# Loading two row tiles as one pair, both halves of wv on ScalarE's queue behind a write of zeros, and v in another order

## The chip, the cores and the metric

The kernel runs on one core of a Trainium2 chip. The metric is the device time of one execution in microseconds (us); the time before is the median of 3 runs. One further execution was recorded by the hardware profiler; all times inside the kernel are from that one, counted from its first instruction.

## What is computed

x is 2048 rows of 512 (bf16). It is layer-normed and goes through two branches whose results are added to x: a linear attention with 32 heads of 16, and a gated product of 1792 columns.

```
def _A_ref(x, wqkv, w_phi, wo):
    ...
    q, k, v = qkv[0], qkv[1], qkv[2]
    pq = jnp.einsum("bhsd,hdf->bhsf", q, w_phi)
    pk = jnp.einsum("bhsd,hdf->bhsf", k, w_phi)
    phi_q = jnp.concatenate([_softmax(pq, axis=-1), _softmax(-pq, axis=-1)], axis=-1)
    phi_k = jnp.concatenate([_softmax(pk, axis=-1), _softmax(-pk, axis=-1)], axis=-1)
    kv = jnp.einsum("bhsf,bhsd->bhfd", phi_k, v)
    z  = jnp.einsum("bhsf->bhf", phi_k)
    num = jnp.einsum("bhqf,bhfd->bhqd", phi_q, kv)
    den = jnp.einsum("bhqf,bhf->bhq", phi_q, z)[..., None] + 1e-6
    ...
def _B_ref(x, w_gate, w_up, w_down):
    ...
    h = g * u
    return jnp.einsum("bsf,fd->bsd", h, w_down)
x = A_x
xn = _layernorm(x, axis=-1)
return x + _A_ref(xn, A_wqkv, A_w_phi, A_wo) + _B_ref(xn, B_w_gate, B_w_up, B_w_down)
```

Attention sums k and v over all rows, and the rest treats each row by itself. So any assignment of rows to tiles gives the same result, if the output rows go back to the same places.

## The kernel before

The 2048 rows are 16 tiles of 128 rows (one row per partition) in four groups of four; `xall` holds them all. The order of instructions on each engine is the order in which the program is written (a manual schedule), so what is written earlier on an engine's queue goes first.

**Loads.** x0 and x2 (tiles 0 and 2) and the second half of the weight `wv` (`dma_wv(2, DC)`, L84) are issued first on SyncE's queue (SP), in that order; x1 and the first half of `wv` on ScalarE's queue (ACT, L91 and L92); x3 on GpSimd's (POOL, L93). Behind them SP issues the first 256 columns of the two gate weights `wg` and `wu`, the small `wphi`, their next pieces, a transposing load of a weight, further rows of x, and the rest (L94 to L103).

**First four tiles.** TensorE (PE) runs warm-up matmuls on constants (L307 to L313) while the loads are under way. For tile n, the row sum is made (`sum_of` on VectorE for tiles 0 and 3; on ScalarE with an accumulating activation, L378, for 1 and 2), and `sub_sum` (VectorE, L338) writes 512 x - sum, the centred row. `lt` (L203) transposes it on PE in four 128x128 pieces and a copy (VectorE or ScalarE, L207) puts the pieces into `xnT`. `first_v` (L354, matmuls at L237) multiplies with `wv`: four matmuls, the first two with the first half of `wv`, the others with the second. The variance is taken later (`stats_of`, `scales_of`, L341 to L348, VectorE and GpSimd), and the scale is put on where v is copied out (`first_v_out`) and in the exponentials. Then GpSimd makes `bd`, the block-diagonal form of `w_phi` (`make_bd`, L213), and PE goes into the gated branch (`ffn`, L266: four g matmuls at L275, four u matmuls at L279 per unit), three units, before `fold(1, W1k)` (L226) multiplies `w_phi` into the weights of k and needs `bd`.

The order of the first four tiles is written out at L376 to L405. On PE it is: transposes of tile 0, of tile 1, v of tile 0 (first half of `wv`), transposes of tile 2, v of tiles 1 and 2 (first half), v of tile 0 (second half), transposes of tile 3, v of tiles 1 and 2 (second half), v of tile 3.

**The rest.** Tiles 4 to 15 are normalised by VectorE, GpSimd and ScalarE and transposed by DMA (`ln_block`); k's features, v and their sums kv alternate with units of the gated branch (L435 to L452); then queries, attention and the final products `fin` (L285), whose results SP writes to `out` (L302).

Of the kernel before, what the change touches and what calls it, by code (L numbers as in the profile page):

```python
# [21 lines left out]
def kernel(  # L22
# [12 lines left out]
    nc = tc.nc  # L35
    P = 128
    S, D = A_x.shape[-2], A_x.shape[-1]
# [3 lines left out]
    NT = S // P  # L41
    DC = D // P
# [4 lines left out]
    TT = GT * P  # L47
    E1 = DH + 1

    x_view = A_x.flatten_outer_dims().rearrange("(n p) d -> p n d", n=NT)  # L50
    out_view = out.flatten_outer_dims().rearrange("(n p) d -> p n d", n=NT)

    consts = ctx.enter_context(tc.tile_pool(name="consts", bufs=1))
    wpool = ctx.enter_context(tc.tile_pool(name="wpool", bufs=1))
# [2 lines left out]
    xall = xpool.tile([P, NT, D], BF16)  # L57
    wv = wpool.tile([P, DC, D], BF16)
# [9 lines left out]
    def dma_x(lo, hi, eng=nc.sync):  # L68
        eng.dma_start(out=xall[:, lo:hi, :], in_=x_view[:, lo:hi, :])
# [4 lines left out]
    def dma_wv(lo, hi, eng):  # L74
        eng.dma_start(out=wv[:, lo:hi, :],
                      in_=A_wqkv[lo * P:hi * P, 2 * D:3 * D].rearrange("(c p) f -> p c f", p=P))

    def dma_gu(lo, hi):
        dma_cols(nc.sync, wg, B_w_gate, lo, hi)
        dma_cols(nc.sync, wu, B_w_up, lo, hi)  # L80

    dma_x(0, 1)
    dma_x(2, 3)
    dma_wv(2, DC, nc.sync)  # L84

    ET = mybir.EngineType
    ctx.enter_context(tc.manual_schedule(engines={ET.PE, ET.DVE, ET.Activation, ET.Pool, ET.SP}))
    ones = nc.const_aps.tensor(1.0, [P, P], BF16)
    first = consts.tile([P, 1], BF16)
    nc.scalar.activation(out=first[:], in_=ones[:, 0:1], func=AF.Exp, scale=1.0)  # L90
    dma_x(1, 2, nc.scalar)  # L91
    dma_wv(0, 2, nc.scalar)  # L92
    dma_x(3, 4, nc.gpsimd)  # L93
    dma_gu(0, 2 * P)  # L94
    nc.sync.dma_start(out=wphi[:], in_=A_w_phi.rearrange("(c h) d f -> (h d) c f", c=DC))
# [27 lines left out]
    xnT = xpool.tile([P, DC, S], BF16)  # L123
# [22 lines left out]
    def bank(name, dt=F32, n=TT):  # L146
        return ps_s.tile([P, n], dt, name=name, tag="s")
# [52 lines left out]
        for i in range(GT):  # L200
            chores.append(lambda i=i: apply(i))

    def lt(n, lo=0, hi=DC, copy=nc.scalar.copy):  # L203
        tp = bank("tp", BF16).rearrange("p (c t) -> p c t", c=DC)
        for c in range(lo, hi):
            nc.tensor.transpose(out=tp[:, c, :], in_=xns[n][:, c * P:(c + 1) * P], identity=ident[:])  # L206
        copy(out=xnT[:, lo:hi, n * P:(n + 1) * P], in_=tp[:, lo:hi, :])  # L207

    bd = consts.tile([P, DC, 8, DH], BF16)

# [24 lines left out]
    def proj(ps, n, w, js=range(DC)):  # L235
        for j in js:
            nc.tensor.matmul(ps, lhsT=xnT[:, j, n * P:(n + 1) * P], rhs=w[:, j, :],  # L237
                             start=(j == 0), stop=(j == DC - 1))
# [46 lines left out]
    def fin(n, cuts=(0, D)):  # L285
        T, t4 = n // GT, n % GT
        for lo, hi in zip(cuts, cuts[1:]):
            w = hi - lo
            ps = bank("fin")[:, 0:w]
            for f in range(FC):  # L290
                nc.tensor.matmul(ps, lhsT=hTs[T][:, f, t4 * P:(t4 + 1) * P], rhs=wd[:, f, lo:lo + w],  # L291
                                 start=(f == 0), stop=False)
            for c in range(DC):
                nc.tensor.matmul(ps, lhsT=oTs[n][:, c, :], rhs=wo[:, c, lo:lo + w],  # L294
                                 start=False, stop=(c == DC - 1))
            o_sb = opool.tile([P, w], BF16, name=f"o_sb{w}")
            if n < GT:
                nc.vector.scalar_tensor_tensor(out=o_sb[:], in0=ps, scalar=r2[n][:], in1=xall[:, n, lo:lo + w],
                                               op0=ALU.mult, op1=ALU.add)
            else:  # L300
                nc.vector.tensor_tensor(out=o_sb[:], in0=ps, in1=xall[:, n, lo:lo + w], op=ALU.add)  # L301
            nc.sync.dma_start(out=out_view[:, n, lo:lo + w], in_=o_sb[:])  # L302


    warm = bank("warm")
# [1 line left out]
    def warm_up(k, reps=DC):  # L307
        for _ in range(k):
            nc.tensor.matmul(warm[:, 0:reps * P], lhsT=ones,
                             rhs=nc.const_aps.tensor(1.0, [P, reps * P], BF16), start=True, stop=True)  # L310

    warm_up(7)
    warm_up(2, 1)  # L313

    with tc.tile_pool(name="ps_k", bufs=1, space=PSUM) as ps_k:
        kvbank = [ps_k.tile([P, TT], F32, name=f"kv{b}") for b in range(2)]
# [20 lines left out]
        def sub_sum(n, tot, lo=0, hi=D):  # L337
            nc.vector.tensor_scalar(out=xns[n][:, lo:hi], in0=xall[:, n, lo:hi], scalar1=float(D), scalar2=tot[:],  # L338
                                    op0=ALU.mult, op1=ALU.subtract)
# [14 lines left out]
        def first_v(n, js):  # L354
            if n not in vps:
                vps[n] = kvbank[n][:] if n < 2 else bank("pv")
            proj(vps[n], n, wv, js)
# [15 lines left out]
        def sum_of(n):  # L373
            nc.vector.tensor_reduce(out=tots[n][:], in_=xall[:, n, :], axis=AX.X, op=ALU.add)  # L374
# [3 lines left out]
            nc.scalar.activation(out=junk[:], in_=xall[:, n, :], func=AF.Identity, accum_out=tots[n][:])  # L378
        sub_sum(0, tots[0], 0, D // 2)
        sub_sum(0, tots[0], D // 2, D)  # L380
        sub_sum(1, tots[1])
        lt(0, 0, 2, nc.vector.tensor_copy)
        lt(0, 2, DC, nc.vector.tensor_copy)
        lt(1, 0, 2)
        sub_sum(2, tots[2])
        lt(1, 2, DC, nc.vector.tensor_copy)
        first_v(0, (0, 1))
        lt(2, 0, 2)
        sum_of(3)
        lt(2, 2, DC, nc.vector.tensor_copy)  # L390
        sub_sum(3, tots[3])
        first_v(1, (0, 1))
        first_v(2, (0, 1))
        first_v(0, (2, 3))
        lt(3)
        first_v(1, (2, 3))
        first_v(2, (2, 3))
        for n in (2, 3, 0, 1):
            stats_of(n)
            scales_of(n, float(D))  # L400
# [58 lines left out]
    with tc.tile_pool(name="ps_ab", bufs=1, space=PSUM) as ps_ab, \  # L459
# [23 lines left out]
        for n in range(NT):  # L483
            attend(n)
            if n + 5 < NT:
                qproj(n + 5)
            if n < 2:
                ffn(2)
                continue
            fin(n - 2)  # L490
            if n >= 4:
                ffn(2)
        ffn(len(units))
        fin(NT - 2)
        fin(NT - 1, (0, 3 * P, D))


# [28 lines left out]
```

## Time and profile before

| what | before |
|---|---|
| median of 3 runs | 220.36 us (220.27 to 220.91) |
| the profiled execution | 220.46 us |
| its span, first to last instruction | 218.8 us |
| PE busy | 214.9 us (98%) |
| VectorE, ScalarE, GpSimd busy | 141.0, 89.2, 74.9 us |
| x0 issued, landed | 0.79 us, 3.24 us |
| first transpose on PE | 4.34 us |
| first matmul of the gated branch | 9.34 us |
| data moved by DMA | 19.91 MB |

A line of the profile names the engine, the line of the kernel, the operation, and the tile written with those read. PE is TensorE's matmuls, PEld its weight loads, DVE is VectorE, ACT ScalarE, POOL GpSimd, SP SyncE; a q behind the name means the engine's issuing side. In the chain of work that ended last, each piece is what the next one waited for. "Landed" is when the last part of a transfer has raised its semaphore.

### The profile page before, as it was taken

What the parts mean: (1) busy time and instruction counts of PE and PEld (TensorE: products, weight loads), DVE (VectorE), ACT (ScalarE), POOL (GpSimd) and SP (SyncE); (2) the same over time, 40 slices, a digit from 0 to 9 for tenths busy, and PEclk for the clock granted to TensorE, in tenths of its full rate; (3) what the DMA queues carried; (4) which work ended last, traced back from release to release, by engine and by line L of the source; (5) the groups of instructions that cost most, each with busy time, mean ns of one, the idle gap of its engine ahead of it and who ended that gap; (6) DMA issues with size and microseconds to landing.
All of it is one profiled execution on the core that took longest, in us unless ns stands there. A gap on an engine that the chain in (4) does not pass through costs nothing.

```text
span 218.8 us, 3493 instructions
## 1 busy us (share of the span) xinstructions
PE 214.9 (98%) x1291; PEld 103.1 (47%) x1291; DVE 141.0 (64%) x242; ACT 89.2 (41%) x159; POOL 74.9 (34%) x72
## 2 busy tenths in 40 slices
PE   8999999999999999999999999999999999999994
PEld 3444445454444444444544444444444444454443
DVE  4878867786598758576599773296655655454321
ACT  5545686569575875565435212141231322100000
POOL 4450843373357554636045333033123033000000
PEclk9999999999999999999999999999999999999999
DMA  5999996005202240202028355114461431412201
GB/s 198 286 297 372 372 219 136 2 0 51 48 0 49 51 94 2 48 3 48 1 43 105 76 114 114 37 24 96 96 70 30 95 72 28 96 48 72 69 30 48
DMA packets 48433, 19.91 MB, mean 91 GB/s; under 512 B 37504, under 2 KB 48384, under 8 KB 48416
## 3 DMA queue, kind: packets, MB, share of 16 engines
q1 hardware_dynamic: 47952, 19.16, 38.9%
q10 hardware_dynamic: 416, 0.39, 0.5%
q8 instruction: 10, 0.16, 0.3%
q0 software_dynamic: 48, 0.13, 0.2%
q14 instruction: 7, 0.06, 0.1%
HBM read 8.67 MB, written 2.10 MB: 49 GB/s over the span
## 4 chain that ended last, share of the span: by engine, by line
PE 97%; DMA 1%; DVE 1%; issue 0%
PE g L275 22%; PE fin L291 22%; PE u L279 22%; PE fin L294 6%; PE q L237 6%; PE k L237 6%; PE pv L237 6%; PE kv L331 2%; PE ab L465 2%; DMA xall<-in_A_x_dram 1%; PE kv L237 1%; PE tp L206 1%; PE pq L226 1%; DVE tot L374 0%; DVE xn L338 0%; DVE o_sb L301 0%
## 5 line engine op out<-in xcount | busy, mean ns | idle before, releaser
L275 PE MATMUL g<-xnT,wg 128*128 128x512 bf16 x224 | 57.5, 379 | 0.0
L279 PE MATMUL u<-xnT,wu 128*128 128x512 bf16 x224 | 57.5, 379 | 0.0
L254 POOL TENSOR_TENSOR phiq<-e,rsum 128x1024 bf16<-128x1024 f32 x16 | 30.9, 1933 | 63.5 <-DVE rsum L252 56.0
L283 DVE TENSOR_TENSOR hT<-u,g_sb 128x512 bf16<-128x512 f32 x56 | 37.0, 666 | 23.9 <-PE u L279 15.8
L282 ACT CAST g_sb<-g 128x512 bf16<-128x512 f32 x56 | 32.9, 587 | 46.8 <-PE g L275 46.5
L250 DVE TENSOR_REDUCE sums<-e 128x64 f32<-128x1024 f32 x32 | 38.9, 1216 | 20.1 <-ACT e L247 20.1
L291 PE MATMUL fin<-wd,hT 128*128 128x512 bf16 (+2 forms) x238 | 51.1, 366 | 0.0
L254 POOL TENSOR_TENSOR phik<-e,rsum 128x1024 bf16<-128x1024 f32 x16 | 30.9, 1932 | 39.6 <-DVE rsum L252 33.6
L279 PEld LDWEIGHTS <-wu 128*128 128x128 bf16 x224 | 21.9, 98 | 26.4
L291 PEld LDWEIGHTS <-hT 128*128 128x128 bf16 x238 | 22.4, 98 | 24.8
L275 PEld LDWEIGHTS <-wg 128*128 128x128 bf16 x224 | 21.1, 98 | 24.0
L237 PEld LDWEIGHTS <-xnT 128*128 128x128 bf16 x192 | 17.4, 98 | 18.2 <-ACT xnT L207 0.7
L301 DVE TENSOR_TENSOR o_sb<-fin,xall 128x512 bf16<-128x512 f32 (+2 forms) x13 | 8.5, 651 | 20.5 <-PE fin L294 20.5
L252 DVE RECIPROCAL rsum<-sums 128x64 f32<-128x64 f32 x32 | 17.7, 553 | 3.1
L294 PE MATMUL fin<-wo,oT 128*128 128x512 bf16 (+2 forms) x68 | 16.6, 366 | 0.0
L237 PE MATMUL k<-W1k,xnT 128*128 128x512 bf16 x64 | 16.4, 379 | 0.0
L237 PE MATMUL q<-W1q,xnT 128*128 128x512 bf16 x64 | 16.4, 378 | 0.0
L246 ACT ACTIVATE e<-q 128x512 f32<-128x512 f32 x12 | 7.2, 597 | 22.2 <-PE q L237 22.2
L237 PE MATMUL pv<-wv,xnT 128*128 128x512 bf16 x56 | 14.4, 379 | 0.0
L478 DVE TENSOR_TENSOR otok<-ab,rden 128x512 bf16<-128x512 f32 x16 | 11.1, 692 | 0.6
L323 ACT CAST vt<-pv 128x512 bf16<-128x512 f32 x12 | 7.0, 587 | 10.0 <-PE pv L237 10.0
L154 DVE BATCH_NORM_STATS2 stats<-xall 128x6 f32<-128x512 bf16 x16 | 10.6, 664 | 0.0
(63 smaller groups left out, 131.8 us busy)
## 6 DMA issues: line engine op xcount, KB each, us to landing
out_dram<-o_sb SPq DMA_DIRECT2D x15, 128.0 KB, 2.0
wd<-in_B_w_down_dram SPq DMA_DIRECT2D x1, 1792.0 KB, 15.8
xall<-in_A_x_dram SPq DMA_DIRECT2D x1, 1024.0 KB, 11.9
wg<-in_B_w_gate_dram SPq DMA_DIRECT2D x1, 640.0 KB, 7.7
wu<-in_B_w_up_dram SPq DMA_DIRECT2D x1, 640.0 KB, 10.4
xall<-in_A_x_dram SPq DMA_DIRECT2D x1, 512.0 KB, 4.5
wg<-in_B_w_gate_dram SPq DMA_DIRECT2D x1, 512.0 KB, 5.3
wu<-in_B_w_up_dram SPq DMA_DIRECT2D x1, 512.0 KB, 6.4
```

The lines of the kernel that those rows point to most:

```text
L154: nc.vector.bn_stats(out=stats[:], in_=xall[:, n, :])
L237: nc.tensor.matmul(ps, lhsT=xnT[:, j, n * P:(n + 1) * P], rhs=w[:, j, :], start=(j == 0), stop=(j == DC - 1))
L250: nc.vector.tensor_reduce(out=sums[:], in_=ev, axis=AX.X, op=ALU.add)
L252: nc.vector.reciprocal(out=rsum[:].rearrange("p a b -> p (a b)"), in_=sums[:])
L254: nc.gpsimd.tensor_tensor(out=phi[:].rearrange("p g (x f) -> p (g x) f", f=DH), in0=ev, in1=rsum[:].to_broadcast((P, 2 * H, DH)), op=ALU.mult)
L275: nc.tensor.matmul(gps, lhsT=wg[:, c, f * P:(f + 1) * P], rhs=xnT[:, c, T * TT:(T + 1) * TT], start=(c == 0), stop=(c == DC - 1))
L279: nc.tensor.matmul(ups, lhsT=wu[:, c, f * P:(f + 1) * P], rhs=xnT[:, c, T * TT:(T + 1) * TT], start=(c == 0), stop=(c == DC - 1))
L282: nc.scalar.copy(out=g_sb[:], in_=gps)
L283: nc.vector.tensor_tensor(out=hTs[T][:, f, :], in0=ups, in1=g_sb[:], op=ALU.mult)
L291: nc.tensor.matmul(ps, lhsT=hTs[T][:, f, t4 * P:(t4 + 1) * P], rhs=wd[:, f, lo:lo + w], start=(f == 0), stop=False)
L294: nc.tensor.matmul(ps, lhsT=oTs[n][:, c, :], rhs=wo[:, c, lo:lo + w], start=False, stop=(c == DC - 1))
L478: nc.vector.tensor_tensor(out=o_tok[:].rearrange("p (b h d) -> p b h d", b=2, d=DH), in0=abv[:, :, :, 0:DH], in1=rden[:].to_broadcast((P, ...
```

## The change

Tiles 1 and 2 become a pair: partition p holds rows 128 + 2p and 128 + 2p + 1, which lie behind one another in memory (2 KB). One transfer on SP, straight behind x0, loads both; x1 leaves ScalarE's queue. The outputs of the two tiles go to the same rows.

Both halves of `wv` are issued on ScalarE's queue. VectorE first writes zeros into a part of `wv`'s first half, so the transfer of that half has to wait for this write; the second half is behind it on the queue.

`lt` returns its copy instead of issuing it, so that the copy's place among VectorE's instructions can be chosen. The first four tiles are reordered: on PE transposes of tile 0, v of tile 0 (first half), transposes of tile 1, v of tile 0 (second half), transposes of tile 2, all of v of tile 1, transposes of tile 3, all of v of tile 2, then v of tile 3. One of the two short warm-up matmuls goes.

```
+    x_rows, out_rows = A_x.flatten_outer_dims(), out.flatten_outer_dims()
+    PAIR = 1
+    def pair(rows):
+        return rows[PAIR * P:(PAIR + 2) * P, :].rearrange("(p j) d -> p j d", j=2)
+    def out_of(n, lo, hi):
+        if n in (PAIR, PAIR + 1):
+            return pair(out_rows)[:, n - PAIR, lo:hi]
+        return out_view[:, n, lo:hi]
...
     dma_x(0, 1)
-    dma_x(2, 3)
-    dma_wv(2, DC, nc.sync)
+    nc.sync.dma_start(out=xall[:, PAIR:PAIR + 2, :], in_=pair(x_rows))
...
-    dma_x(1, 2, nc.scalar)
+    nc.vector.memset(wv[:, 0, 0:D // 2], 0.0)
     dma_wv(0, 2, nc.scalar)
+    dma_wv(2, DC, nc.scalar)
     dma_x(3, 4, nc.gpsimd)
...
-    def lt(n, lo=0, hi=DC, copy=nc.scalar.copy):
+    def lt(n, lo=0, hi=DC):
...
-        copy(out=xnT[:, lo:hi, n * P:(n + 1) * P], in_=tp[:, lo:hi, :])
+        return lambda copy: copy(out=xnT[:, lo:hi, n * P:(n + 1) * P], in_=tp[:, lo:hi, :])
...
-            nc.sync.dma_start(out=out_view[:, n, lo:lo + w], in_=o_sb[:])
+            nc.sync.dma_start(out=out_of(n, lo, lo + w), in_=o_sb[:])
...
     warm_up(7)
-    warm_up(2, 1)
+    warm_up(1, 1)
...
         sub_sum(0, tots[0], D // 2, D)
+        lt(0, 0, 2)(nc.vector.tensor_copy)
+        later = lt(0, 2, DC)
         sub_sum(1, tots[1])
-        lt(0, 0, 2, nc.vector.tensor_copy)
-        lt(0, 2, DC, nc.vector.tensor_copy)
-        lt(1, 0, 2)
-        sub_sum(2, tots[2])
-        lt(1, 2, DC, nc.vector.tensor_copy)
+        later(nc.vector.tensor_copy)
         first_v(0, (0, 1))
-        lt(2, 0, 2)
+        lt(1, 0, 2)(nc.scalar.copy)
+        later = lt(1, 2, DC)
+        sub_sum(2, tots[2])
+        later(nc.vector.tensor_copy)
+        first_v(0, (2, 3))
+        lt(2, 0, 2)(nc.scalar.copy)
+        later = lt(2, 2, DC)
         sum_of(3)
-        lt(2, 2, DC, nc.vector.tensor_copy)
         sub_sum(3, tots[3])
-        first_v(1, (0, 1))
-        first_v(2, (0, 1))
-        first_v(0, (2, 3))
-        lt(3)
-        first_v(1, (2, 3))
-        first_v(2, (2, 3))
+        later(nc.vector.tensor_copy)
+        first_v(1, range(DC))
+        lt(3)(nc.scalar.copy)
+        first_v(2, range(DC))
```

More of the change, by code (lines that the diff above doesn't have):

```diff
@@ L48 @@
     E1 = DH + 1
-    x_view = A_x.flatten_outer_dims().rearrange("(n p) d -> p n d", n=NT)
-    out_view = out.flatten_outer_dims().rearrange("(n p) d -> p n d", n=NT)
+    x_rows, out_rows = A_x.flatten_outer_dims(), out.flatten_outer_dims()
+    x_view = x_rows.rearrange("(n p) d -> p n d", n=NT)
+    out_view = out_rows.rearrange("(n p) d -> p n d", n=NT)
+    PAIR = 1
[5 more added lines that the diff above has]
+        return out_view[:, n, lo:hi]
     consts = ctx.enter_context(tc.tile_pool(name="consts", bufs=1))
@@ L380 @@
         sub_sum(0, tots[0], D // 2, D)
+        lt(0, 0, 2)(nc.vector.tensor_copy)
+        later = lt(0, 2, DC)
         sub_sum(1, tots[1])
-        lt(0, 0, 2, nc.vector.tensor_copy)
-        lt(0, 2, DC, nc.vector.tensor_copy)
-        lt(1, 0, 2)
+        later(nc.vector.tensor_copy)
+        first_v(0, (0, 1))
+        lt(1, 0, 2)(nc.scalar.copy)
+        later = lt(1, 2, DC)
         sub_sum(2, tots[2])
-        lt(1, 2, DC, nc.vector.tensor_copy)
-        first_v(0, (0, 1))
-        lt(2, 0, 2)
+        later(nc.vector.tensor_copy)
+        first_v(0, (2, 3))
+        lt(2, 0, 2)(nc.scalar.copy)
+        later = lt(2, 2, DC)
         sum_of(3)
-        lt(2, 2, DC, nc.vector.tensor_copy)
         sub_sum(3, tots[3])
-        first_v(1, (0, 1))
-        first_v(2, (0, 1))
-        first_v(0, (2, 3))
-        lt(3)
-        first_v(1, (2, 3))
-        first_v(2, (2, 3))
+        later(nc.vector.tensor_copy)
+        first_v(1, range(DC))
+        lt(3)(nc.scalar.copy)
+        first_v(2, range(DC))
         for n in (2, 3, 0, 1):
```

## The prediction

> **What bounds the kernel now.** I read the page first: the busy shares, then the chain that ended last. Both say that the end is set by TensorE alone.
>
> ```profile
> PE 214.9 (98%) x1291; PEld 103.1 (47%) x1291; DVE 141.0 (64%) x242; ACT 89.2 (41%) x159; POOL 74.9 (34%) x72
> ...
> PE 97%; DMA 1%; DVE 1%; issue 0%
> ```
>
> PE is busy in 98% of the span and the chain is PE for 97%; the remaining 2% lies ahead of PE's first useful instruction. In the records of the matmuls I find no hole after 4.34 us except 0.08 us at 6.43 us and a few of 0.1 us where PE goes over to or comes from the folds. So a change near the start is worth exactly what it shifts the first gated-unit matmul (g, L275), now at 9.34 us: all behind it is queued on PE and moves along. The diff touches nothing behind that point but two output writes. I therefore read the chain in order of time over the first 9.6 us.
>
> ```profile
> 0.79 2.45 DMA xall<-in_A_x_dram
> 3.25 0.02 issue
> 3.27 0.70 DVE tot L374
> 3.97 0.03 issue
> 3.99 0.30 DVE xn L338
> 4.29 0.05 issue
> 4.34 1.07 PE tp L206 x8
> 5.40 0.54 PE kv L237 x2
> ```
>
> The first row is x0, issued at 0.79 us and landed at 3.24 us; then its row sums, its centring, and PE starts 1.09 us after the landing. Then the timeline of PE:
>
> ```profile
> 4.34 1.07 PE L206 MATMUL tp<-ident,xn 128*128 128x128 bf16 x8
> 5.20 0.74 PE L237 MATMUL kv<-wv,xnT 128*128 128x512 bf16 x2
> 5.78 0.39 PE L206 MATMUL tp<-ident,xn 128*128 128x128 bf16 x4
> ```
>
> Eight transposes take 1.07 us and four take 0.39 us: in the single records they start 0.107 us apart up to 5.09 us and 0.056 us from 5.78 us. The first kv matmul has 0.36 us to the next, later ones 0.216 us, so PE goes from half to full speed at about 5.48 us (the PEclk row has 9 throughout and doesn't show it). Two things follow. PE work done before 5.48 us counts half: an earlier start of 0.25 us is worth 0.12. And from 5.48 us on PE is nearly dense, so the most that any rearrangement can win is small.
>
> The landings come from the DMA view of this stretch (its last column is us from issue to landing):
>
> ```profile
> wv<-in_A_wqkv_dram ACTq DMA_DIRECT2D x1, 256.0 KB, 3.4
> wv<-in_A_wqkv_dram SPq DMA_DIRECT2D x1, 256.0 KB, 4.4
> ...
> xall<-in_A_x_dram ACTq DMA_DIRECT2D x1, 128.0 KB, 2.7
> xall<-in_A_x_dram POOLq DMA_DIRECT2D x1, 128.0 KB, 4.1
> ```
>
> With the issue times of the timeline and the landing records: x1 (ScalarE, 0.85) at 3.55 us, x2 (SyncE, 1.25) at 3.91, first half of wv (ScalarE, 1.28) at 4.64, x3 (GpSimd, 1.29) at 5.41, second half of wv (SyncE, 1.71) at 6.15, first piece of wg (SyncE, 2.18) at 7.08. They land in the order of their issue, 128 KB in 0.30 to 0.37 us.
>
> **The change, part by part.** "T0" is the four transposes of row tile 0, and so on.
>
> *x0.* x1 no longer goes out beside x0. x0's 16 completions came in two lots, 4 at 2.63 to 2.67 us and 12 at 3.00 to 3.25, and x1's packets began at 2.20. Bounds for the landing: 2.79 (0.79 + the 2.0 us of the 128 KB output writes) and 3.24 (now). I take the middle, 3.0. T0 then starts at 3.0 + 1.09 = 4.09 and ends at 4.09 + 4 x 0.107 = 4.52. The warm-up matmul that goes (0.107 us) is hidden: the warm-up now ends 0.15 us ahead of T0 and will end at about 4.08.
>
> *Write of zeros.* DVE's first instruction at 0.86 us is a memset. The rows of 4 elements (0.062 us) and 32 elements (0.085 to the 0.13 that they are apart) give about 0.2 us for this one (128 words). So ScalarE issues wv at about 1.1 us instead of 1.28, and the second half at about 1.55 instead of 1.71. DVE idles 1.64 us before x0 lands; that hides the 0.2.
>
> *The pair.* The same 256 KB on SyncE at 1.25 us, in 128 packets instead of 256; wv's first half goes out slightly ahead of it. No row shows 2 KB packets here. Bounds by the places in the queue now: 3.55 (straight behind x0) and 4.64 (behind wv's first half). I take 3.95, near x2's 3.91, since the bytes are the same. ScalarE starts the sum of row tile 1 0.02 us after the landing, and the centring of it (DVE) starts 0.82 us after that (3.57 to 4.39 now): 4.79 to 5.14; that of tile 2 follows 0.75 later, 5.54 to 5.89.
>
> *New order on DVE and PE.* T0's first copy on DVE starts 0.43 us after T0 (4.34 to 4.77 now): 4.52 to 4.81. v of tile 0, first half, starts 0.14 us behind that (copy's end 5.06, matmul 5.20 now): 4.95. PE idles 0.43 us, in half-speed time; T1 filled it before. The first matmul takes 0.43 us at half speed, the second ends at 5.64 across the change of clock. T1 needs the centring (5.14), so it follows at once: 5.64 to 5.86. Then v of tile 0, **second half**, now third on PE and not eighth: before, it started at 6.96, 0.8 us after wv's second half had landed; now PE reaches it at 5.86.
>
> *Second half of wv.* Bounds: 5.1 (wv's first half's 4.64 less x0's 0.25, plus 0.73 for 256 KB, nothing beside it) and 7.08 (the landing of wg's first piece, if that goes ahead). I take 6.1, what it has now, since the same bytes lie ahead of it. PE waits from 5.86 to 6.15, 0.29 us, and everything on PE is queued behind.
>
> *To g.* v of tile 0 ends at 6.58; T2 (centred at 5.89) 6.80; v of tile 1, 4 x 0.216, 7.67. DVE meanwhile: T1's second copy 6.03 to 6.31, sums of tile 3 to 6.99 (x3 landed at 5.41), its centring 7.02 to 7.36, T2's second copy to 7.64. So T3 starts unhindered, 7.67 to 7.89, then v of tiles 2 and 3, 8 x 0.216, 9.62. **g starts at 9.62 instead of 9.34: +0.28 us.** Without the wait for wv it would be 9.33, no change.
>
> *What is hidden.* The statistics on DVE start at 7.64 and not 6.70, and GpSimd's chain behind them with the block-diagonal matrix bd moves by as much:
>
> ```profile
> 12.57 1.07 POOL L213 TENSOR_TENSOR bd<-BO,wphi 128x512 bf16<-128x512 bf16 x1
> ```
>
> It now ends at 13.65 and will at 14.59; the fold that needs it starts at 14.61 now and at 14.89 then. Hidden by 0.3 us; it also forbids a gain of more than 0.1 us unless DVE is earlier too. The multiplies that DVE does late (hT of the first two units) are waited for by the fold's banks only, which have the same slack. SyncE loses one transfer (0.47 us) ahead of wg, wu and wphi; these have over 2 us to spare. Its second piece of wu then waits for x0 and the weight transpose for the pair; both land before SyncE is there. Outputs of tiles 1 and 2 keep 128 rows of 1 KB and are not at the end.
>
> **Sum.** The profiled execution took 220.46 us (span 218.8, so 1.66 around it), 0.10 above the median of the runs. 220.46 + 0.28 = 220.74, or 220.64 in terms of the median. I say 220.6.
>
> **Rivals.**
> 1. *wv's second half comes in time* (by 5.8 us), for x0 is sooner out of the way: g at 9.33, or at 9.2 with x0 at 2.8 and dense work: 220.2 to 220.4. For: bytes ahead are no more than now, and it is issued 0.16 us earlier. Against: x3 lands in the same stretch, as now.
> 2. *The change doesn't hold wv back.* The zeros delay it to about 1.1 us only, x1's old 0.85 being near; if x0 still lands at 3.24, PE would reach v's second half at 5.99, and the wait for wv at 6.15 makes the same 220.6, or 220.5 without it.
> 3. *Slower: wg goes ahead of wv's second half.* Before, both were on SyncE's queue, in order; now they are on different queues and wg is free to start behind the pair. The DMA view of 3.6 to 4.4 us shows one queue held while the other drained:
>
> ```profile
> q10 hardware_dynamic: 186, 0.17, 62.2%
> q0 software_dynamic: 32, 0.11, 44.5%
> q1 hardware_dynamic: 4, 0.00, 1.8%
> ```
>
> q1 (SyncE) moved 4 packets though wv's second half had been issued at 1.71; q10 (ScalarE) had its turn. If wg has its turn likewise, wv lands as late as 7.08 and g starts at 10.55: +1.2, 221.6. It decides from a landing of 6.5 on (6.55 - 5.86 = 0.7 us of waiting). Against: wv is issued about 0.15 us before wg. The Trainium skill (DMA: Bandwidth & Descriptors, Queues, rings and completion order) says that each DMA engine takes turns between the queues that have work, a packet of several descriptors at a time; by that rule wg and wv would share the engines and wv would land between 6.1 and 7.1. The rows above agree with taking turns, in pieces as large as a whole transfer.
> 4. *The clock rises later*, because PE idles 0.43 us before 5.48; the idle time before T0 is 0.15 us now. From the first warm-up matmul (0.83) to the change of speed it is 4.65 us. If that count began anew at 4.95, the change would come at 9.6 and not at 5.48; 4.1 us more at half speed cost 2.05 us, in which the wait for wv disappears: 220.36 + 2.05 = 222.4. Against: the stretch from 0.83 has 0.15 us of idling now and the change comes all the same; no row shows how much more it bears. The Trainium skill (TensorE: Matmul & The Clock Gate, Part 1) has a free-running window of about 3.4 us of activity that releases the clock; by that figure the price would be about 1.7 us.
>
> **Chances.** What a measurement here can tell from no change is about 0.3%, 0.66 us (219.70 to 221.02). The forecast (wait of 0.1 to 0.6 us) 0.45; rivals 1 and 2 without a wait 0.25; rival 3 with 0.66 us or more 0.19; rival 4 0.05; faster by over 0.66 us 0.06, which on these rows only an earlier clock could give. So faster 0.06, same 0.70, slower 0.24. The range 220.1 to 221.4 leaves out rival 4, rival 3 at its full price and the faster case, about 0.16 together.
>
> **What would show it.** Landing of x0 at about 3.0; T0 at 4.1; PE idle 0.4 us before v's first matmul at 4.95; PE waiting for the DMA of wv (not for DVE) at about 5.9 to 6.15; g at 9.6; no idle time of PE at the fold (14.9). Wrong if wv lands by 5.8 (g at 9.33 or before), if the pair lands after 4.5 (then T1 and T3 wait for centring), if wg lands before wv, or if transposes after 5.5 us are still 0.107 us apart.

## The result and the profile after

The changed kernel takes 221.44 us (median of 12 runs, 221.03 to 222.71) and the kernel before 220.46 (12 runs on the same chip, 220.27 to 220.95): a ratio of 1.0051 with a 95% interval of 1.0034 to 1.0068. It is slower by about 1.0 us, where 0.2 us had been forecast. The profiled execution took 221.43 us, close to that median; its span is 219.7 us.

The busy shares and the chain of the changed kernel, from the page:

```profile
PE 215.3 (98%) x1290; PEld 102.7 (47%) x1290; DVE 141.3 (64%) x243; ACT 89.1 (41%) x159; POOL 75.0 (34%) x72
...
PE 96%; DMA 2%; ACT 0%; DVE 0%; SPq 0%; issue 0%
```

PE still sets the end, but the part of the chain that is not PE now goes through the pair and ScalarE. In order of time (start, us, what; 217 is now the line of the copies, 247 of the v matmuls, 348 of the centring, 388 of ScalarE's row sum):

```profile
1.25 4.13 DMA xall<-in_A_x_dram
5.38 0.02 issue
5.40 0.73 ACT junk L388 x2
...
6.16 0.36 DVE xn L348
6.52 0.05 issue
6.56 0.40 PE tp L216 x4
```

The pair lands at 5.38 us, 4.13 us after its issue. Sum, centring and the transposes T1 follow without a pause. PE in the same stretch, from its timeline (start, us, then in brackets what ended the idle time before):

```profile
5.17 1.01 PE L247 MATMUL kv<-wv,xnT 128*128 128x512 bf16 x2 [0.55 <-DMA wv<-in_A_wqkv_dram]
6.56 0.40 PE L216 MATMUL tp<-ident,xn 128*128 128x128 bf16 x4 [0.38 <-DVE xn L348]
6.92 0.59 PE L247 MATMUL kv<-wv,xnT 128*128 128x512 bf16 x2
...
10.46 1.03 PE L285 MATMUL g<-xnT,wg 128*128 128x512 bf16 x4
```

PE waits for wv's first half (landed 5.13), then for T1's centring. The first g matmul starts at 10.46 instead of 9.34: +1.12, and 221.43 - 10.46 = 210.97 lies behind it, against 211.12 before. In all profiled executions of this study 210.95 to 211.14 us lie behind the start of that matmul, whatever was changed. So the whole loss is made ahead of g, as the forecast had it; only its size is in question.

The other landings: x0 at 2.93, wv's second half at 6.88, x3 at 5.76, wg at 7.39. Where the time is lost is seen in the DMA view of 2.8 to 3.6 us, first of the kernel before, then of the changed one:

```profile
DMA packets 317, 0.29 MB, mean 364 GB/s; under 512 B 33, under 2 KB 317, under 8 KB 317
```

```profile
DMA packets 119, 0.15 MB, mean 187 GB/s; under 512 B 1, under 2 KB 91, under 8 KB 119
```

Behind x0 the engines move half of what they moved before. In slices of 0.2 us from 2.6 on the rates are 138, 102, 133, 241 and 271 GB/s (before: 343, 364, 348, 379, 364), and single packets of wv take up to 722 ns, where the usual 1 KB packet takes 46. I call this stretch **the gap**. That is not the same as idling. The time that packets take fills this share of the 16 engines (last number of each line; 2.8 to 3.6 us, first before, then changed):

```profile
q10 hardware_dynamic: 174, 0.17, 60.7%
q1 hardware_dynamic: 143, 0.13, 45.6%
```

```profile
q10 hardware_dynamic: 91, 0.09, 58.8%
q1 hardware_dynamic: 28, 0.06, 19.3%
```

Together 78%, where it was 106% (packets overlap). So the engines have packets for a quarter less of the time, and in that time move 30% less.

### The profile page after: what moved, and what is told of

It reads as the page before. It is cut to its first block, busy times and chain, and to the rows that moved or that the text cites. A ratio compares the mean times of both kernels' runs of the same rounds, so it can differ in the third digit from the quotient of the medians.

```text
span 219.7 us, 3488 instructions
## 1 busy us (share of the span) xinstructions
PE 215.3 (98%) x1290; PEld 102.7 (47%) x1290; DVE 141.3 (64%) x243; ACT 89.1 (41%) x159; POOL 75.0 (34%) x72
## 4 chain that ended last, share of the span: by engine, by line
PE 96%; DMA 2%; ACT 0%; DVE 0%; SPq 0%; issue 0%
PE g L285 22%; PE fin L301 22%; PE u L289 22%; PE fin L304 6%; PE q L247 6%; PE k L247 6%; PE pv L247 6%; DMA xall<-in_A_x_dram 2%; PE kv L341 2%; PE ab L476 2%; PE kv L247 1%; PE pq L236 1%; PE tp L216 0%; ACT junk L388 0%; SPq L79 0%; DVE xn L348 0%
```

## The experiments

"wv1" and "wv2" are the halves of wv; "v0b" is v of tile 0, second half, which needs T1 to be done and wv2 to have landed. Landings and starts are those of the one profiled execution (us); times are medians, and the kernel before took 220.44 to 220.86 beside them. The ratios are not those of the two medians (touch_wg_later: 221.13 over 220.65 would be 1.0022). A profiled execution need not lie at its median: loads_only's took 224.50, wv_later's 224.30, pair_1k's 221.26 and touch_wv's 221.53. Most intervals overlap that of the changed kernel; so what an edit does to the path is read from the start of g, in one execution each.

| kernel | time | ratio to before [95%] | wv1 | pair | wv2 | v0b | g |
|---|---|---|---|---|---|---|---|
| changed | 221.44 | 1.0051 [1.0034, 1.0068] | 5.13 | 5.38 | 6.88 | 6.92 | 10.46 |
| order_only | 221.13 | 1.0031 [1.0013, 1.0049] | 5.15 | x1 3.57, x2 4.07 | 6.04 | 6.08 | 9.54 |
| loads_only | 223.36 | 1.0126 [1.0106, 1.0146] | 5.04 | 5.38 | 6.90 | | 13.51 |
| loads_only_fill | 221.62 | 1.0048 [1.0028, 1.0068] | 4.94 | 5.12 | 6.87 | | 10.64 |
| after_fill | 221.76 | 1.0050 [1.0027, 1.0074] | 4.90 | 5.09 | 6.52 | 6.56 | 10.17 |
| pair_1k | 222.84 | 1.0087 [1.0059, 1.0116] | 4.77 | 5.22 | 6.65 | 6.69 | 10.30 |
| wv_later | 222.62 | 1.0084 [1.0046, 1.0123] | 6.21 | 4.13 | 7.56 | 7.60 | 13.30 |
| one_queue | 222.65 | 1.0094 [1.0065, 1.0124] | 6.10 | 3.70 | 6.89 | 7.38 | 11.61 |
| no_zeros | 220.99 | 1.0031 [0.9994, 1.0068] | 3.91 | 4.55 | 5.28 | 5.97 | 9.63 |
| zeros_small | 221.39 | 1.0047 [1.0025, 1.0069] | 4.34 | 5.00 | 6.50 | 6.55 | 10.08 |
| x3_first | 225.34 | 1.0215 [1.0173, 1.0257] | 5.17 | 4.77 | 8.75 | 8.79 | 14.57 |
| pair_on_act | 220.93 | 1.0038 [1.0009, 1.0067] | 4.89 | 3.93 | 6.19 | 6.23 | 9.69 |
| touch_wv | 222.40 | 1.0061 [1.0014, 1.0108] | 5.08 | 4.35 | 6.88 | 6.93 | 10.39 |
| touch_x | 221.54 | 1.0052 [1.0019, 1.0085] | 5.03 | 4.22 | 6.86 | 6.90 | 10.36 |
| wg_later | 222.72 | 1.0078 [1.0046, 1.0110] | 5.86 | 5.67 | 6.76 | 7.09 | 12.23 |
| touch_wg_later | 221.13 | 1.0004 [0.9972, 1.0036] | 5.14 | 4.51 | 6.11 | 6.37 | 9.86 |

### The order or the transfers

**order_only** keeps the transfers of before, with the new order on PE and DVE:

```
-    nc.sync.dma_start(out=xall[:, PAIR:PAIR + 2, :], in_=pair(x_rows))
+    dma_x(2, 3)
+    dma_wv(2, DC, nc.sync)
...
-    nc.vector.memset(wv[:, 0, 0:D // 2], 0.0)
+    dma_x(1, 2, nc.scalar)
     dma_wv(0, 2, nc.scalar)
-    dma_wv(2, DC, nc.scalar)
```

> The transfers of the kernel before, with the new order of PE and VectorE (and one short warm-up matmul less). Theory L (the loss comes from the loads: the pair lands at 5.4 us and not at 3.9): x1, x2 and both halves of wv land as before (3.5, 3.9, 4.6, 6.1), v of tile 0, second half, waits for wv to 6.15 us, g starts at about 9.6, 220.6 to 220.8 us. Rival O (the loss comes from the order: PE idles and its clock rises later): 221.2 us or more, g after 10.1.

Measured: close to the forecast's schedule. PE waits for wv2 (6.04) as forecast for 6.15, and g starts at 9.54 (forecast 9.62). One landing is not as before: wv1 comes at 5.15 instead of 4.64, by the same transfers, and T0 is followed by a wait for it. This execution has a dip behind x0 too: 236, 164 and 241 GB/s in the slices from 2.8 to 3.4 us (before: 364, 348, 379), and 1 KB packets of up to 581 ns. So a landing in this stretch can differ by 0.5 us between two executions of the same transfers, and the dip is not the new transfers' alone. The median is 0.5 us above before, the profiled execution, 220.66, only 0.2. By g the new order costs its 0.2 us and the whole change 1.12; by the medians' intervals, which overlap, the order's share of the loss is not told apart.

**loads_only** has the new transfers with the order of before:

```
-        lt(0, 0, 2)(nc.vector.tensor_copy)
-        later = lt(0, 2, DC)
         sub_sum(1, tots[1])
-        later(nc.vector.tensor_copy)
-        first_v(0, (0, 1))
-        lt(1, 0, 2)(nc.scalar.copy)
+        lt(0, 0, 2, nc.vector.tensor_copy)
+        lt(0, 2, DC, nc.vector.tensor_copy)
+        lt(1, 0, 2)
...
```

> The new transfers, with the order of the kernel before. Theory L: the pair lands at about 5.4 us, PE idles for it behind the transposes of tile 0, as all of v is queued behind the transposes of tile 1; g at 10.5 or later, 221.4 us or more. Rival O: g at 9.4 to 9.6, 220.4 to 220.6 us.

Measured: the largest loss but one. Here T1 comes second on PE and waits for the late pair from 4.41 to 6.57; the landings are those of the changed kernel. So the transfers alone make a loss, a larger one than the whole change, and the new order makes it smaller: it gives PE v of tile 0 to do.

### The clock

**loads_only_fill**: five useless matmuls (on constants) fill that wait.

```
         lt(0, 2, DC, nc.vector.tensor_copy)
+        warm_up(5)
         lt(1, 0, 2)
```

> The new transfers with the old order (loads_only), and five warm-up matmuls of 512 columns written behind the transposes of tile 0, where PE idled 2.2 us. Theory C (the idling keeps PE at half speed for one or two more steps of 3.41 us; in loads_only the clock rose at 12.3 us): the clock rises by 9 us at the latest, g starts at 10.5 to 11, 221.4 to 222.0 us instead of 223.36, and the runs lie closer. Rival (all the loss is waiting for the pair): no change, 223.2 us or more.

Measured: 1.7 us less than loads_only, by work that computes nothing. PE's timeline, first of loads_only, then with the filling:

```profile
6.57 0.61 PE L216 MATMUL tp<-ident,xn 128*128 128x128 bf16 x4 [1.96 <-DVE xn L348]
6.97 1.06 PE L247 MATMUL kv<-wv,xnT 128*128 128x512 bf16 x2
```

```profile
6.31 0.40 PE L216 MATMUL tp<-ident,xn 128*128 128x128 bf16 x4 [0.20 <-DVE xn L348]
6.54 0.59 PE L247 MATMUL kv<-wv,xnT 128*128 128x512 bf16 x2
```

The same four transposes take 0.61 us in the one and 0.40 in the other. In the trace's record of the granted clock the rise to full speed is at 12.34 us in loads_only and at 5.21 with the filling. That is what rival 4 said, a clock that rises later because PE idled. In these two executions g starts 2.87 us apart (13.51 and 10.64), of which the pair's landing, 5.38 and 5.12, makes 0.26; the medians are 1.74 us apart.

**after_again** is the changed kernel once more, in one further profiled execution.

> The changed kernel once more, for its landings and its clock in another execution. Theory Q and T: the pair at 5.1 to 5.4, wv at 4.9 to 5.1 and 6.5 to 6.9 again, since four executions with these transfers had that; the clock rises at another time than 6.1 us. 221.0 to 222.7 us.

It took 222.95 us, 1.5 more than the first profiled execution, with nearly the same landings (wv1 5.24, pair 5.42, wv2 6.79):

```profile
6.61 0.61 PE L216 MATMUL tp<-ident,xn 128*128 128x128 bf16 x4 [0.31 <-DVE xn L348]
7.01 1.06 PE L247 MATMUL kv<-wv,xnT 128*128 128x512 bf16 x2
```

Half speed again (the first had 0.40 and 0.59), until 10.01 us; g starts at 11.96. So the changed kernel's slowest runs, up to 222.71 in the 12, are read as executions with a late clock; this one is shown to be.

**after_fill** puts two useless matmuls behind T0 and two behind v of tile 0, first half, of the changed kernel:

```
         later = lt(0, 2, DC)
+        warm_up(2)
...
         first_v(0, (0, 1))
+        warm_up(2)
```

> The changed kernel, with two warm-up matmuls of 512 columns behind the transposes of tile 0 and two behind v of tile 0, first half, where PE idled 0.75 and 0.6 us. Theory C: its slowest runs (222.2 to 222.7) go, median 220.9 to 221.3 us with a spread under 0.8 us. Rival (the spread comes from the transfers alone): the same median and spread as the changed kernel, 221.0 to 222.7 us.

Missed: the median is no better (221.76). Only the runs above 222.2 are gone. A clock that rises in time, at 3.97 in the profiled execution, leaves g at 10.17 all the same. So a clock that rises too late does not explain the 1.0 us of the medians.

### Why the data are late

**pair_1k** loads the same two tiles, by the same queue and at the same time, in 256 packets of 1 KB:

```
-    nc.sync.dma_start(out=xall[:, PAIR:PAIR + 2, :], in_=pair(x_rows))
+    dma_x(PAIR, PAIR + 2)
```

> The changed kernel, with rows 128 to 383 loaded by one transfer as two tiles in their natural rows, 256 packets of 1 KB and not 128 of 2 KB. Theory K (packets of 2 KB are what is slow beside wv's): the pair lands at 4.6 us or sooner, about 220.8 us. Theory Q (wv's first half, issued 0.16 us ahead, takes turns with the pair or goes first, whatever the packet): it lands at 5 us or later, 221.2 us or more.

The pair lands at 5.22, hardly earlier, and g starts at 10.30; the median, 222.84, is higher than the changed kernel's, and no trace here says why. The packets of 2 KB are not the cause; undisturbed ones take 84 ns, 42 per KB.

**wv_later** writes zeros into all of wv1, so that wv goes out at 1.49 us:

```
-    nc.vector.memset(wv[:, 0, 0:D // 2], 0.0)
+    nc.vector.memset(wv[:, 0:2, :], 0.0)
```

> The changed kernel, with zeros written to all of wv's first half, so that the write takes some 0.35 us longer and ScalarE issues wv at about 1.45 us, behind the pair's 1.25. Theory Q: the pair lands before wv, at 3.6 to 4.1 us, wv at 4.6 and about 6; 220.4 to 220.9 us. Theory K: the pair lands at 4.8 or later, 221.2 us or more.

The pair comes at 4.13, as expected by the theory of a queue in which wv lay ahead of it; but wv1 lands at 6.21 where 4.6 was expected. 0.4 us later out, 1.1 us later in.

**one_queue** has no zeros and puts wv behind the pair on SyncE:

```
+    dma_wv(0, 2, nc.sync)
+    dma_wv(2, DC, nc.sync)
...
-    nc.vector.memset(wv[:, 0, 0:D // 2], 0.0)
-    dma_wv(0, 2, nc.scalar)
-    dma_wv(2, DC, nc.scalar)
```

> The changed kernel, with both halves of wv issued by SyncE straight behind the pair, and no write of zeros. Theory Q (wv on ScalarE's queue gets ahead of the pair or takes turns with it): the pair lands at 3.6 to 4.1 us, wv at 4.4 to 4.8 and 5.2 to 5.7, g at 9.2 to 9.5, 220.2 to 220.7 us. Rival S (transfers as large as the pair start slowly, whatever is beside them): the pair at 4.5 us or later, 221 us or more.

The pair lands at 3.70 as expected, wv1 only at 6.10, though it waits for no write and nothing is on ScalarE's queue. A stretch of low rates is now at 3.4 to 4.0 us (87 to 225 GB/s). Its long packets, up to 1121 ns, are of 4 KB on GpSimd's queue, which carries x3. So wv1 can be late without the write and without ScalarE's queue; that this stretch has the same cause as the gap is not shown.

**no_zeros** only takes the write of zeros away, so that wv goes out at 0.85 and 1.31 us:

```
-    nc.vector.memset(wv[:, 0, 0:D // 2], 0.0)
```

> The changed kernel without the write of zeros, so that ScalarE issues wv at about 0.85 us. Theory Q: wv's first half is beside x0, x0 lands at 3.2 us or later and the pair no sooner than now (5.2 us or later), 221.4 us or more. Rival S: x0 at 2.9 and the pair at 5.4 as in the changed kernel, the same time.

Both theories missed: everything comes early, and there is no gap (at least 277 GB/s from 2.4 us on). g starts at 9.63, as forecast, and the profiled execution took 220.62; the median, 220.99, is 0.4 above before, and its interval reaches to both sides of no change. **zeros_small** writes two columns, and wv goes out at 0.95:

```
-    nc.vector.memset(wv[:, 0, 0:D // 2], 0.0)
+    nc.vector.memset(wv[:, 0, 0:2], 0.0)
```

> The changed kernel with zeros written to 2 columns and not 256, so that ScalarE issues wv at about 0.96 us, between no_zeros (0.85) and the changed kernel (1.09). Theory T (what counts is how early wv's descriptors are asked for: issued at 0.85 its first half landed at 3.9, at 1.09 at 4.9 to 5.1, at 1.49 at 6.2): wv lands at 4.2 to 4.7, the pair at 4.6 to 5.0, about 221.2 us. Rival W (any wait ahead of wv's issue does it): wv at 4.9 to 5.1 and the pair at 5.1 to 5.4 as in the changed kernel. Rival: as no_zeros, 3.9 and 4.5.

wv1 at 4.34 and the pair at 5.00 lie between the other two, and the gap is short, as expected. With nothing else ahead on its queue, wv1 issued at 0.85, 0.95, 1.09 and 1.49 us landed at 3.91, 4.34, 4.77 to 5.86 and 6.21: **the landing moved by about four to eight times the delay of the issue behind 0.85** (0.24 us later out, 0.86 to 1.95 later in). All but the third are one execution each.

**x3_first** keeps the engines supplied with x3 in the place of the zeros:

```
-    nc.vector.memset(wv[:, 0, 0:D // 2], 0.0)
+    dma_x(3, 4, nc.scalar)
...
-    dma_x(3, 4, nc.gpsimd)
```

> The changed kernel with x3 on ScalarE's queue at 0.85 us, where the write of zeros stood, and nothing on GpSimd's; wv's halves follow on ScalarE at 1.28 and 1.74 us. Theory T (late issue alone): wv's first half as late as with 1.09 or later, 5 us or more, 221.2 us or more. Rival F (a queue that is fed from 0.85 us on stays fast, as in the kernel before, where wv was issued at 1.28 behind x1): x0 3.2, x3 3.5, pair 4.2, wv 4.6 to 4.9 and 5.4 to 5.9, 220.4 to 220.9 us.

Rival F missed. Theory T's bounds hold (wv1 at 5.17, over 221.2 us), but not because of wv1: x3 lands early (3.64), and PE waits 2.12 us for wv2, which lands together with wg at 8.75. **pair_on_act** exchanges the queues: x0 and wv on SyncE, the pair first on ScalarE at 0.85 us.

```
+    dma_wv(0, 2, nc.sync)
+    dma_wv(2, DC, nc.sync)
...
-    nc.vector.memset(wv[:, 0, 0:D // 2], 0.0)
-    dma_wv(0, 2, nc.scalar)
-    dma_wv(2, DC, nc.scalar)
+    nc.scalar.dma_start(out=xall[:, PAIR:PAIR + 2, :], in_=pair(x_rows))
```

> The changed order with x0 and then both halves of wv on SyncE, and the pair on ScalarE at 0.85 us. Rival F: x0 at 3.1, pair at 3.8 to 4.0, wv at 4.5 to 4.8 and 5.2 to 5.7; g at 9.3 to 9.6, 220.3 to 220.8 us. Theory T: the pair at 3.9, but wv (issued at 1.25 and 1.71) at 5.3 or later, 221 us or more.

The pair lands at 3.93, g starts at 9.69. Theory T missed (wv1 at 4.89); rival F was right on the pair and a little early on the rest. The median is the lowest of the versions with a pair, 0.5 us above before, but its interval overlaps theirs.

### Two delays, each enough

**touch_wv** puts a transfer of 16 pieces of 64 B ahead of wv on ScalarE's queue, read from wv1's rows; **touch_x** the same from rows of x that are loaded later. The tile is read by nothing.

```
+    touch = consts.tile([16, 32], BF16)
+    nc.scalar.dma_start(out=touch[:], in_=A_wqkv[0:2 * P, 2 * D:2 * D + 32].rearrange("(p j) f -> p j f", j=16)[:, 0, :])
     nc.vector.memset(wv[:, 0, 0:D // 2], 0.0)
```

```
+    nc.scalar.dma_start(out=touch[:], in_=x_rows[8 * P:10 * P, 0:32].rearrange("(p j) f -> p j f", j=16)[:, 0, :])
```

> The changed kernel with one more transfer ahead of wv on ScalarE's queue, issued at about 0.85 us: 16 pieces of 64 B out of the rows of wv's first half, into a tile that nothing reads. Theory R (the first packets of a queue are slow, and in the changed kernel ScalarE's first use falls where nothing else is under way): the slow packets go into the tiny transfer, wv lands at 4.0 to 4.6 us, the pair at 4.4 to 4.8, the rate at 2.6 to 3.2 us is above 250 GB/s, the time 220.7 to 221.1. Theory W (the first reading of wv's memory is slow): the same here. Theory N (only the issue time of the large transfers counts): as the changed kernel or worse, pair 5.1 to 5.5, 221.4 to 221.8.

> As touch_wv, but the 16 pieces of 64 B come out of rows 1024 to 1279 of x, which are otherwise loaded much later. Theory R: as touch_wv, pair at 4.4 to 4.8 and 220.7 to 221.1. Theory W: not mended, pair at 5.1 to 5.5, packets of wv of over 300 ns again, 221.4 to 221.8. Theory N: not mended in either.

The pair came at 4.35 and 4.22, on time, and neither run is faster than the changed kernel. The tiny transfer also moves wv's issue from 1.09 to 1.28 us, behind the pair's 1.25; so why the pair is on time is not isolated. The gap stayed, though shorter (down to 62 and 113 GB/s in a slice of 0.2 us), and its slow packets, up to 687 ns, are now those of the pair, which has taken wv1's place behind x0. So the gap isn't due to wv's memory, nor to the first use of a queue; theories R and W fall, and theory N's landings of the pair (5.1 to 5.5) missed too. What makes the loss now is seen in PE's timeline of touch_x:

```profile
5.70 0.39 PE L218 MATMUL tp<-ident,xn 128*128 128x128 bf16 x4
6.90 0.59 PE L249 MATMUL kv<-wv,xnT 128*128 128x512 bf16 x2 [0.81 <-DMA wv<-in_A_wqkv_dram]
...
10.36 0.81 PE L287 MATMUL g<-xnT,wg 128*128 128x512 bf16 x3
```

T1 at 5.70 is as forecast (5.64), then PE waits for wv2, which lands at 6.86; wg, issued on the other queue, lands before it, at 6.79. That is rival 3. In the DMA view of the changed kernel from 4.8 to 6.2 us the two queues have half of the engines each:

```profile
q1 hardware_dynamic: 462, 0.24, 55.6%
q10 hardware_dynamic: 232, 0.22, 47.3%
```

q10 (ScalarE) has wv2, q1 (SyncE) mostly wg. In no_zeros, from 4.4 to 5.0, wv2 drains while wg, issued 0.4 us behind it, stands:

```profile
q10 hardware_dynamic: 139, 0.13, 60.4%
q0 software_dynamic: 31, 0.12, 49.8%
q1 hardware_dynamic: 3, 0.00, 0.8%
```

Two runs hold wg back. **wg_later** is the changed kernel with SyncE's transfers from wg on, in the same order, behind a write to wg's tile:

```
         sub_sum(0, tots[0], D // 2, D)
+        nc.vector.memset(wg[:, 0, 0:2], 0.0)
+        dma_gu(0, 2 * P)
...
```

**touch_wg_later** does the same to touch_x.

> The changed kernel, but SyncE's transfers from wg's first piece on are issued behind a write of two zeros per partition into wg's tile, by VectorE behind the centring of tile 0 (at about 4.0 us). Nothing then shares the engines with wv's second half. Theory D (two delays, each enough): wv's second half lands at 5.5 to 6.1 us, but the pair still at 5.1 to 5.4, so the first gated-unit matmul comes at 10.0 to 10.4 and the time is 221.1 to 221.5. Theory P (the pair's lateness is the only delay that counts): the same time here. Theory S (only the sharing counts): 220.5 to 220.9.

> touch_x and wg_later together: the tiny transfer of 64 B pieces of x ahead of wv, and wg held back. Theory D: the pair at 4.2 to 4.6 us, wv's second half at 5.5 to 6.1, the first gated-unit matmul at 9.5 to 9.8 as forecast, and 220.5 to 220.9 where the clock rises by 5.5 us. Theory P is already at odds with touch_x, and theory S gives the same time here as in wg_later. If wv's second half lands after 6.5 though wg is held back, sharing isn't what delays it and theory D falls: 221.2 to 221.6.

wg_later missed: its profiled execution had a longer gap (82 to 205 GB/s until 3.4 us; wv1 5.86, pair 5.67) and the clock at half speed from 7.40 to 10.81 us. It does not separate the two delays. touch_wg_later lands wv2 at 6.11 instead of 6.86, at the edge of what was expected:

```profile
5.18 1.01 PE L239 MATMUL kv<-wv,xnT 128*128 128x512 bf16 x2 [0.44 <-DMA wv<-in_A_wqkv_dram]
5.99 0.54 PE L208 MATMUL tp<-ident,xn 128*128 128x128 bf16 x4
6.37 0.59 PE L239 MATMUL kv<-wv,xnT 128*128 128x512 bf16 x2
...
9.86 1.03 PE L277 MATMUL g<-xnT,wg 128*128 128x512 bf16 x4
```

No wait for wv2 is left; g starts at 9.86, 0.06 us beyond the expected 9.5 to 9.8, because wv1 lands at 5.14 and T1 still runs mostly at half speed (0.54 us). The time, 221.13, is beyond the expected 220.5 to 220.9, though the interval now reaches to both sides of no change. So with the pair on time, taking the sharing away is worth 0.50 us of g (10.36 to 9.86); taking the pair's delay away alone (touch_x) is worth 0.10. No run isolates the pair's delay with wv2 on time; what it does alone is worked out below from traces.

## Why the prediction was wrong

By the forecast's own steps:

- *The path.* Right: TensorE ahead of g, and nothing behind it. The rest after g is constant within 0.2 us in all these runs.
- *x0.* Right: 2.93 (forecast 3.0), in one lot of completions; T0 at 4.02 (4.09).
- *Write of zeros.* Right in itself: wv goes out at 1.09 and 1.57 (1.1 and 1.55). Costed at the delay that it makes, it was mis-sized: without it wv1 lands at 3.91, with it at 5.13.
- *The pair.* **Failed**: "I take 3.95", bounds 3.55 to 4.64; 5.38 was measured, and 5.09 to 5.42 in the four other profiled executions with exactly these transfers. This is the sign that the forecast had named itself ("if the pair lands after 4.5"). The bounds were places in the queue of before, and in that one trace the rate does not drop at this point. The gap and the mixing with wv1 had no row there; order_only shows that by the transfers of before, too, another execution can have a dip and wv1 0.5 us later. And of the landings read as "128 KB in 0.30 to 0.37 us", x3's took 0.77 (4.64 to 5.41).
- *wv1.* The step reads v of tile 0 as starting when DVE's copy is done (4.95), and gives wv1 no landing of its own; it was 4.64 before. It lands at 5.13, and PE starts at 5.17.
- *Second half of wv.* **Failed**: "I take 6.1, what it has now, since the same bytes lie ahead of it"; 6.88 was measured. The bytes ahead are the same, but it shares the engines with wg, which is now on another queue than wv2 and goes out 0.47 us earlier (1.71 instead of 2.18), which the forecast had noted only as time to spare. By the forecast's own working this alone gives the result: v0b at 6.92 and 3.47 us from there to g make 10.39, or 220.36 + 1.05 = 221.4. And the pair alone gives nearly the same. v0b itself waited 0.12 us for wv2 (T1 was done at 6.80), but T2 needs the pair's second tile: in pair_1k and after_fill, where v0b was done 0.04 us before, T2 started 1.94 us after the pair's landing. In the changed kernel that makes 5.38 + 1.94 = 7.32, and T2 started at 7.35, when v0b was done. The two delays end within 0.03 us of each other, so either hides the other, and the profile after names only the pair.
- *New order and the sum.* Right for the path: g was forecast at 9.62. order_only has it at 9.54, and no_zeros, where wv2 is in time and PE waits 0.23 us for the pair's centring, at 9.63; its profiled execution took 220.62, where 220.74 was forecast for one. The medians of the two (221.13 and 220.99) lie above the forecast's 220.64. From v0b to g it is 3.46 to 3.66 us in all runs at full speed.
- *Rival 3* (wg with wv2) was the nearest, and was given 0.19. It had said 221.6 for a landing at 7.08. What it set against itself, that wv goes out ahead of wg, was no help in the changed kernel (1.57 and 1.71); in no_zeros (1.31 and 1.71) wv2 drained first. The rule cited beside it, that an engine takes turns between the queues that have work (the Trainium skill, DMA: Bandwidth & Descriptors, Queues, rings and completion order), agrees with the shares 55.6% and 47.3%; the view of no_zeros (60.4% and 0.8%) does not look so. What decides between the two stays open.
- *Rival 4* (the clock) is real, at 1.5 us between the two profiled executions of the changed kernel and 1.7 between the medians of loads_only and loads_only_fill, but not what moves the median; 0.05 was too little for what happened in some of the runs. The forecast also took the rise at 5.48 for fixed; in the other executions it came anywhere from 3.97 us to 13.53.

**Open**: why packets take so long behind x0, and with that why the pair is late; for wv2 the sharing is shown (6.86 against 6.11), for the pair no cause is. The gap follows whichever transfer comes next behind the first 128 KB. It was absent or small where a second large transfer was issued by 0.85 us (the kernel before, no_zeros, x3_first, pair_on_act), but order_only, which issues x1 at 0.85, has a dip all the same; so the early issue is not shown to be the cause. The packet size, the first use of a queue and the first reading of wv don't explain it. The engines' records of single packets of 300 to 1000 ns don't say what those waited for. No version here beats the kernel before.

## What to carry to other kernels

Bounds for a landing that come from the places in today's queue are one execution's: the same transfers landed wv1 at 4.64 and at 5.15 here, and a reordered queue had the pair 0.7 us outside them. Ask of every transfer not only what lies ahead of it, but when it is issued, and what on another queue may share its turn. Where a schedule needs two transfers at one point, work out the time by each of them; the profile shows only the later one, and mending it brings the other. A hole at the start of PE's work can cost more than its length, through the clock.

## What was not expected of the hardware

- In the first 3 us an issue that is 0.1 us later landed 0.4 us later (0.85 to 0.95: 3.91 to 4.34, one execution each; the same issue time scattered by 0.5 to 1.1 us), and single packets took 722 ns instead of 46.
- The granted clock changes in steps of 3.413 us: its stretches of full speed are 215.04 or 211.63 us long, 63 or 62 such steps, and in wg_later it was at full speed from 3.98 us, fell to half for exactly one such step from 7.40, behind a step in which PE had waited 1.42 and 0.36 us, and rose again. The window of about 3.4 us in the Trainium skill (TensorE: Matmul & The Clock Gate, Part 1) agrees with this. How busy PE must be in a step is not shown. If each matmul counts from its start to the next one's, at most for its time in a dense row (at half speed 0.107 us for 128 columns, 0.43 for 512), the least busy step with a rise behind it was filled to about 70% (the changed kernel), and steps filled up to 70% (wv_later) had none. The profile's busy time does not separate them either: 2.87 of 3.41 us ahead of the rise in the changed kernel, 2.85 and no rise in x3_first. Where the steps lie differs from execution to execution (in the two of the changed kernel the rise came at 6.10 and 10.01), and one kernel has runs 1.5 us apart by it.
